# A new issue table, loads spread, minima given anew to POOL or ScalarE, and a ring of 1536 columns, in an attention and ELU kernel

## The chip, the cores and the metric

The kernel runs on one core of a Trainium2 chip. TensorE (PE; its weight loads are listed as PEld), VectorE (DVE), ScalarE (ACT), GpSimd (POOL) and SyncE (SP, which here only issues transfers) each work through a queue of their own, in its order, and wait for each other through semaphores. The metric is the device time of one execution in microseconds; for a kernel the median of its runs is given.

## The reference

Attention over a sliding window, and then two matrix products with an ELU between them. Cut to what matters:

```python
batch, n_heads, seq, head_dim = (8, 8, 576, 64)
scores = scale * np.matmul(q, k.transpose(0, 1, 3, 2))
mask = (rel >= 0) & (rel < 128)
scores = np.where(mask, scores + bias[None], -1e9)        # bias = -slope(head) * |rel|
attn = np.exp(scores - max) / (sum + 1e-09)
x = (attn @ v) as [4608, 512]                             # heads side by side
h = x @ w_in                                              # [4608, 2048]
g = np.where(h > 0.0, h, np.exp(np.minimum(h, 0.0)) - 1.0)
out = g @ w_out                                           # [4608, 512], float32
```

## The kernel before, in words

*Attention.* A batch is worked in four units (keys in blocks of 128, each with up to 256 queries). For batches 2 to 7 a unit is one run of score matmuls on four groups of 32 rows (`scores`, its matmuls recorded at L222), three exponentials on ScalarE (`expo`, L230 and L233) and two products with the table of bias and mask on VectorE (`weigh`, L238). Then come the products with v (`values`, `all_values`, L250 and L271); a column of ones beside v gives the sums. VectorE takes the reciprocal and writes a normalised block of x (`xn`). Batches 0 and 1 take a quicker way in (L136 to L213): their q and k are turned by TensorE, their bias is added by matmuls (L167, L184), and their scores use 64 rows (L177, L192).

*x turned.* The first layer needs x with its 512 features down the partitions. `xT` is a ring of columns, one column a token; a token's place is its number modulo RING, 1728 before. The first nine blocks are turned by TensorE and copied (`turn_x`); the other 31 by a transposing transfer from SyncE's queue (`turn`, L287), which also issues the stores of the output.

*First layer.* 144 hidden steps, each one PSUM bank (`hp`) of 512 values: from step 32 on, 256 tokens by two of the 16 feature groups, in eight matmuls of 256 columns (L312). A step that runs over the ring's end is cut in two pieces (`cuts` in `hidden`), and each piece has matmuls of its own. Steps share two banks in turn, so that step n+2 waits until step n's bank has been read. The ELU is max(exp(min(h, 0)) - 1, h), and exp(min(h, 0)) comes in two ways: by ScalarE alone (relu of -h, L319, then exp of its negative, L321), or by ScalarE's exp (L323) and then the minimum with 1 on POOL (L325). The set SOFT says which step goes which way. VectorE finishes (`elu`, L333), reading `e` and the bank, and frees the bank.

*Second layer.* For every 256 tokens seven products of half matrices instead of eight (Strassen's way): `product` (L403), eight matmuls for one product; the sums of g that they need on VectorE (`sums`, L364: S1 to S4), their results kept by ScalarE (`keep`, L410) and put together by VectorE (`combine`, `lower`, L364).

*Loads.* POOL issues them all: per batch eight pieces of q and k into a staging tile (`load_qk`, L108) and five of v (`load_v`, L114). POOL's minima stand in the same queue.

*The order* is written out. Each kind of work has a queue of jobs; SCRIPT is a text whose letters are taken one by one, and each letter issues the next job of its kind. What each engine does, and in which order, follows from it alone. The letters: f and fA/fD turn q and k of the first batches and copy them; b, i, j are their bias, scores and exponentials; k scores; x, y, z exponentials; w, W products with the table; v, r, n values, reciprocal, block of x; t, tA/tD and T turn x; h, p, q, e are a hidden step's matmuls, its first pass, its second pass and its end; s1 to s4 sums; o one matmul of a product, u its keeping; c and m put together and store; l the next load; C four copies of table parts.

Of the kernel before, what the change touches and what calls it, by code (L numbers as in the profile page):

```python
# [18 lines left out]
def kernel(  # L19
# [15 lines left out]
    RING = 3 * S  # L35
# [114 lines left out]
    with tc.manual_schedule():  # L150
# [369 lines left out]
        for b in range(2, B):  # L520
# [16 lines left out]
        SOFT = {15 + 8 * n + d for n in range(2, 2 * NTB) for d in (0, 1, 2, 3, 4, 7)} | set(range(11, 19)) | {20, 22, 23} | set(range(16 * NTB - 10, 16 * NTB + 8))  # L537

        SCRIPT = """
            f fD f fD b f fA f fD C C C C b i j i j j b i j j v r n v r n b t tD v r n v r n  # L540
            h p q t tD f fA
            e h p q i j f fD f fA f fD b b i j i l
            h p q e j j l
            h p q e b i l
            h p q j v r n v r n e l
            h p q t tD b i j e l
            h p q e
            h p q e
# [12 lines left out]
            s2 W l l o1 u o6 v r n i j i j j
            l l o2 c1 o5 v r n
            W W d l o3 u o4 t tA i j v r n
            W l s4 o4 u o3 v r n
            h p q v r n i j d l
            h p q e W t tA d l o5 u o2
            h p q e v r n i j l
            h p q e W t tA l o7 c2
            h p q e v r n i j d l
            h p q e W l o7 u  # L570
            h p q e v r n v r n l c3 m s1
            o1 h o2 p o1 k l q o1 e o1 v y l t tA d o1
            h x r n e o1 T o1 p o4 s2 u
            h q w o2 e o2 z o4 d p o1
            h w q c1 o2 p v e o4 q o1 r
            h s3 u n o2 p o2 e o1 T o1 u k s4 q o1
            h x e d o2 p o3
            h w u q y l o1 z e o4 p o2 d o1
            h d q w l o1 e v p o2 c2 l o1 q o1
            h r n l o1 e o1 T p o2 l o2 s1 o1 q k l u o1 e o1 x  # L580
            h l d o2 p o1 s2 o4 u
            h w q y e o4 z o2 c3 o2 p o2 w m
            h q c1 v u e p o4 s3 o1 q o1
            h r n o2 p o1 e o1 T o1 k q s4 u
            h e x d o3 p o2 w o1
            h y q z l o1 e o1 u o3 p o1 w o2
            h q d l o1 v c2 p e o1 l o2 q o2 r o2 v l u e v o2
            h r l s1 n o2 p o2
            h r T n q n o2 p e k u d o1 q o3
            h x s2 e o2 p o3 w o3 q o1  # L590
            h c1 y e o1 z o2 s3 o2 p o3 w o1
            h u q c3 v m e T o3 u o2 r o1 p s4 o3
            h n q o1 e T o1 p k d u q
            h x l e o2 p o1 w o4 z o1 q
            h c2 y l e o2 p o2 w l o4 q
            h s1 l e o1 v l p o2 r o1 q l
            h n u d o2 p k e q o3 s2 o2 u
            h x e s3 o2 p o3
            h w q c1 y o1 e o4 z o2 c3 o2 p o1 s4
            h m T u w q o4 e v u p o2 r o3 n o1 q o1  # L600
            h T e o3 u k p c3 q
            h x l e o2 p o2 w o3 y o1 q
            h c2 z l e o2 p o2 w l o2
            h q s1 l v e p l o2 r o1 u v d q o1 m l o1
            h e o1 n o1 p o4 v r T q s2 o3
            h u e o1 s3 o1 p o2
            h r n q c1 o2 n p o3 e o1 T o2 q k d u
            h x e s4 o2 p o1
            h w z d q o5 u o2 e o1 p o4 y o2 q o1
            h u w o1 e o1 p o3 v c3  # L610
            h q r n l o2 e p o1 T o2 l o2 s3 q k l u c2
            h x e m l o3 p
            h w l q s1 l o2 z o2 e o3 y o5 p o1 w
            h q s2 v u e p o4 c1 o1 q
            h r n o2 e p o1 T o4 u s4 k q
            h x e d o2 p o3
            h w u q o1 y o1 e o4 p o2 d o1
            h z q u w l o2 p o3 e o2 v q
            h l r e o1 l n o1 p o5 s3 l T q k c2 u l e
            h x l o2 p o1 w o1  # L620
            h l q s1 o1 z o1 e o4 y o2 c3 o2 p
            h w m q s2 o1 v u p o1 v r o1 e o2 q o1 v c1 o3 e o1
            h u n o2 r p o1 T o1 n
            h r q n o2 T p e o3 k u s4 q
            h x e o2 d o1 p o4
            h z w q y e o2 u o2 p o2 w o4 q
            h c2 l e o2 p v l o2 r o2 s1 q o1
            h l u n o1 l o1 e p o1 T o2 k d l q o1
            h x e o2 p o1 w
            h u s2 q o3 z o1 e o4 y o2 c3 o1  # L630
            h p w m q c1 o1 v e o4 u o2 r o1 p
            h n q s3 T k p e o2 q o1 d o3
            h x e o1 s4 u o3 p
            h w z q o3 l u o1 e o2 p o4 y o1 c2 o1 q o1
            h w l v e p l o2 r o2 c3 o1 l o1 u
            h n q l s1 T m o2 p k e l q s3 o1
            h l x e l o1 s2 o1 p o5 d u o2 q o1
            h z e o1 y o2 w o2 p o2
            h w q c1 o2 e p v v q r o2 s4 o1
            h u e o2 n p v o3 r o1 q T o1 n o3 r o1 u o1 n o1  # L640
            h u e T d o1 k p o1 q x
            h e o2 p o1 w o4 y
            h q c2 z l e o2 p o3 w l o3 q
            h s1 l e o2 p v l o2 r o1 u
            h s2 q l n o2 p o2 c3 o3 u e o1 m T q k d
            h x e o2 p o1 w o1
            h q c1 o1 z o1 e o4 y o2 s3 o2 p
            h w q o2 v u e p o3 s4 o1 u o2
            h q r n o2 p o1 e o1 T o1 k q d
            h x e o2 u o1 w o1 p o5 y o1 q o3 z  # L650
            h e c3 o2 p
            h c2 w q o3 p v e u o2 r o1 q o1 m o1 n
            h s1 T o1 k p e u d q o3
            h x s2 e o2 p o4 c1 o1 z o2 s3 o1
            h q y e o3 p o2 w o2 u o2
            h q w e o2 p v s4 o1 u o1 v q r o2 r v
# [191 lines left out]
```

## Time and profile before

| what | value |
|---|---|
| median of three runs | 305.14 us (304.5 to 305.21) |
| span of the profiled execution, first to last instruction | 303.2 us; the page gives no other time for it, and the runs' median lies 1.9 us above |
| granted TensorE clock | 1.000 |
| busy: PE, DVE, ACT, POOL | 296.2, 256.2, 238.2, 109.1 us |
| POOL's minima (L325) | 44, 28.9 us |
| ScalarE's second passes (L321) | 100, 63.6 us |

The page's span is the time on the core; what lies between it and a run's time is start and end around the program. A row of a group gives line, engine, operation, what it writes and reads, shape and count, then busy time and the mean of one in ns, then the idle time of that engine before it and who ended it. A row of the timeline starts with its start and its length in us.

### The profile page before, as it was taken

The numbers are of one execution on the slowest core, as the hardware profiler recorded it, in microseconds if no ns is written. First come the engines' busy times: TensorE is split into PE (matmuls) and PEld (weight loads), VectorE is DVE, ScalarE is ACT, GpSimd is POOL, SyncE is SP. The second block draws the span as 40 slices with busy tenths as digits, with TensorE's granted clock in tenths as the row PEclk, the third lists the DMA queues.
The fourth block names the chain that finished last, engine by engine and source line by source line (L and its number), as shares of the span: only waits on it lengthen the run. The fifth ranks groups of instructions, "written<-read, shape, count | busy, mean of one in ns | idle before, by whom it ended". The sixth has DMA issues, their size and how long they took to land.

```text
span 303.2 us, 9837 instructions
## 1 busy us (share of the span) xinstructions
PE 296.2 (98%) x4074; PEld 255.6 (84%) x4074; DVE 256.2 (85%) x499; ACT 238.2 (79%) x445; POOL 109.1 (36%) x163
## 2 busy tenths in 40 slices
PE   7899999999999999999999999999999999999996
PEld 5688876989888889988888888887899888898885
DVE  5747879989999999799989898989989887885873
ACT  5577688869797888877979888888887888868881
POOL 8947958671534243332534162606000100010000
PEclk9999999999999999999999999999999999999999
DMA  8999999999394949491969695999220301111013
GB/s 99 193 198 201 201 178 192 125 128 101 36 160 72 131 78 119 83 184 21 161 60 130 107 118 66 130 144 125 61 89 2 97 17 54 54 56 43 37 57 118
DMA packets 96941, 32.04 MB, mean 106 GB/s; under 512 B 83968, under 2 KB 92800, under 8 KB 96896
## 3 DMA queue, kind: packets, MB, share of 16 engines
q0 software_dynamic: 75920, 18.36, 66.6%
q1 hardware_dynamic: 20832, 12.98, 18.0%
q8 instruction: 32, 0.52, 0.7%
q14 instruction: 13, 0.11, 0.1%
q10 hardware_dynamic: 144, 0.07, 0.1%
HBM read 36.70 MB, written 9.44 MB: 152 GB/s over the span
## 4 chain that ended last, share of the span: by engine, by line
PE 86%; DVE 4%; DMA 4%; ACT 2%; POOL 2%; issue 1%; POOLq 0%; DVEq 0%; ACTq 0%
PE hp L312 38%; PE op L403 15%; PE av L403 14%; PE spa L222 4%; PE spa L271 3%; DMA VP<-in_v_dram 2%; PE sp L403 2%; PE sp L312 2%; DMA xT<-xn 2%; PE sp L250 1%; DVE g L333 1%; PE op L339 1%; PE spa L339 1%; ACT e L323 1%; DVE xn L259 1%
## 5 line engine op out<-in xcount | busy, mean ns | idle before, releaser
L312 PE MATMUL hp<-xT,wi 128*128 128x256 f16 (+3 forms) x1488 | 144.1, 245 | 0.9 <-DMA xT<-xn 0.4
L312 PEld LDWEIGHTS <-wi 128*128 128x128 f16 x1600 | 120.6, 98 | 15.1 <-issue 3.9
L333 DVE SCALAR_TENSOR_TENSOR g<-e,hp 128x512 f16<-128x512 f32 x138 | 93.9, 681 | 23.4 <-ACT e L321 12.0
L325 POOL TENSOR_SCALAR e<-e 128x512 f32<-128x512 f32 x44 | 28.9, 657 | 151.4 <-ACT e L323 148.6
L319 ACT ACTIVATE e<-hp 128x512 f32<-128x512 f32 x98 | 58.7, 599 | 28.2 <-PE hp L312 22.9
L321 ACT ACTIVATE e<-e 128x512 f32<-128x512 f32 x100 | 63.6, 636 | 2.2
L403 PEld LDWEIGHTS <-S 128*128 128x128 f16 x544 | 51.0, 98 | 6.6 <-issue 1.1
L403 PEld LDWEIGHTS <-g 128*128 128x128 f16 x400 | 37.1, 98 | 5.4 <-issue 1.5
L238 DVE TENSOR_TENSOR EX<-EX,TAB 128x1024 f16<-128x1024 f16 x48 | 33.0, 694 | 2.8 <-ACT EX L233 1.3
L114 POOL DMA_DIRECT2D VP<-in_v_dram x40 | 34.4, 874 | 1.7 <-DMA s<-in_k_dram 1.3
L323 ACT ACTIVATE e<-hp 128x512 f32<-128x512 f32 x40 | 24.2, 605 | 12.1 <-PE hp L312 12.0
L403 PE MATMUL op<-T,S 128*128 128x256 f16 x192 | 29.5, 273 | 0.0
L403 PE MATMUL av<-T,S 128*128 128x256 f16 x176 | 27.0, 273 | 0.0
L233 ACT ACTIVATE EX<-sp 128x512 f16<-128x512 f32 x48 | 27.0, 602 | 0.0
L230 ACT ACTIVATE EX<-spa 128x1024 f16<-128x1024 f32 x24 | 24.5, 1022 | 1.0 <-PE spa L222 0.5
L364 DVE TENSOR_TENSOR S<-g 128x1024 f16<-128x1024 f16 (+2 forms) x35 | 23.1, 666 | 0.3 <-PE op L403 0.2
L403 PE MATMUL op<-wo,g 128*128 128x256 f16 x128 | 20.4, 273 | 0.0
L403 PE MATMUL av<-wo,g 128*128 128x256 f16 x120 | 19.7, 273 | 0.0
L108 POOL DMA_DIRECT2D st<-in_k_dram x24 | 16.3, 687 | 2.9 <-DMA s<-in_q_dram 2.0
L279 DVE TENSOR_TENSOR xn<-spa,rden 128x512 f16<-128x512 f32 x24 | 16.5, 687 | 0.4
L108 POOL DMA_DIRECT2D st<-in_q_dram x24 | 15.9, 666 | 1.3 <-DMA VP<-in_v_dram 1.3
L222 PE MATMUL spa<-QT,KT 32*128 32x256 f16 (+2 forms) x240 | 15.1, 250 | 0.0
(137 smaller groups left out, 381.5 us busy)
## 6 DMA issues: line engine op xcount, KB each, us to landing
out_dram<-ob SPq DMA_DIRECT2D x32, 256.0 KB, 3.2
VP<-in_v_dram POOLq DMA_DIRECT2D x32, 128.0 KB, 6.1
st<-in_k_dram POOLq DMA_DIRECT2D x24, 144.0 KB, 5.3
st<-in_q_dram POOLq DMA_DIRECT2D x24, 144.0 KB, 5.9
wi<-in_moe_w_in_dram POOLq DMA_DIRECT2D x4, 512.0 KB, 11.2
wo<-in_moe_w_out_dram POOLq DMA_DIRECT2D x4, 512.0 KB, 10.8
out_dram<-ob SPq DMA_DIRECT2D x7, 128.0 KB, 1.7
VP<-in_v_dram POOLq DMA_DIRECT2D x8, 64.0 KB, 6.1
```

What stands on the lines that cost most here:

```text
L108: nc.gpsimd.dma_start(st[b][32 * g:32 * g + 32, w, :, :, :, :].rearrange("p h n j d -> p (h n) (j d)"), (q, k)[w][b, 2 * g:2 * g + 2, :, : ...
L114: nc.gpsimd.dma_start(VP[b % 2][0:p, n, :, 0:D], v[b, :, 128 * n:128 * n + p, :].rearrange("h p d -> p h d"))
L222: nc.tensor.matmul(sp[g][:, 256 * h2 + o:256 * h2 + o + n], kt_[b % 2][r, k0:k0 + 255:2], qt_[b % 2][r, c0:c0 + 2 * n - 1:2], start=dh == ...
L233: nc.scalar.activation(unit(b, u)[:, g, :, :], sp[g].rearrange("p (h c) -> p h c", h=2), AF.Exp, scale=0.125)
L238: V.tensor_tensor(out=e, in0=e, in1=TAB[:, int(u == 3), 2 * gp:2 * gp + 2, :, :], op=ALU.mult)
L312: nc.tensor.matmul(p[:, l * w + u0:l * w + u1], w_in_sb[:, c, fc * 128:(fc + 1) * 128], xT[:, c, x0:x0 + u1 - u0], start=(c == 0), stop=(c ...
L319: nc.scalar.activation(e[:, 0:n], p[:, 0:n], AF.Relu, scale=-1.0)
L321: nc.scalar.activation(e[:, 0:n], e[:, 0:n], AF.Exp, scale=-1.0)
L323: nc.scalar.activation(e[:, 0:n], p[:, 0:n], AF.Exp)
L325: nc.gpsimd.tensor_scalar(out=e[:, 0:n], in0=e[:, 0:n], scalar1=1.0, scalar2=0.0, op0=ALU.min, op1=ALU.max)
L333: V.scalar_tensor_tensor(out=gs[t][:, f0:f0 + nf, c0:c0 + w], in0=sh(es.pop((t, c0, f0))), scalar=1.0, in1=sh(hps.pop((t, c0, f0))), op0=A ...
L403: nc.tensor.matmul(o, a[:, j, :], b[:, j, :], start=j == 0 and i in (1, 2, 5), stop=j == 7, skip_group_check=True)
```

## The change

The whole of SCRIPT is written anew, RING becomes 1536, a turned block that runs over the ring's end is split into two transfers, and SOFT becomes a text with a letter for each of the 144 steps in their order: "a" for ScalarE alone, "g" for POOL. "a" stands 44 times, "g" 100 times; before it was 100 and 44. The jobs themselves and their queues stay as they were. A letter that stands for a load is now more often alone between other letters from batch 4 on. The four table copies C stand later.

```diff
-    RING = 3 * S
+    RING = 1536
...
-            nc.sync.dma_start_transpose(out=xT[:, :, o:o + n], in_=x[0:n, :])
+            for r0, r1 in [(0, n)] if o + n <= RING else [(0, RING - o), (RING - o, n)]:
+                c = (o + r0) % RING
+                nc.sync.dma_start_transpose(out=xT[:, :, c:c + r1 - r0], in_=x[r0:r1, :])
...
-        SOFT = {15 + 8 * n + d for n in range(2, 2 * NTB) for d in (0, 1, 2, 3, 4, 7)} | set(range(11, 19)) | {20, 22, 23} | set(range(16 * NTB - 10, 16 * NTB + 8))
+        SOFT = "aggagaaggggaggaaagaagagaggagggggagggggggaggggggagaggggagagggagaggggggggggggggggagggaaggggggaaggggggaagggggggaagagaaggggggggagggggagaggaaaagaagaa"
...
-            h x e o2 p o1 w o4 z o1 q
-            h c2 y l e o2 p o2 w l o4 q
...
+            h p r n k e o2 u u
+            h z l l o6 s1 s2 q e o2
...
-        for s in sorted(HID):
-            parts(hidden(*HID[s], s in SOFT), "h", "p", "q")
+        for n, s in enumerate(sorted(HID)):
+            parts(hidden(*HID[s], SOFT[n] == "a"), "h", "p", "q")
```

Three places of the order, before and then now. The lines of the changed kernel are 2 higher from `turn` on: L335 is `elu`, L327 the minimum, L299 the copy of a turned block.

ScalarE at the start, from the exponentials of the first two score banks on (EX_92 is the second unit, hp_101 and hp_102 the two banks of the first hidden steps, sp_100 and sp_99 two score banks):

```order
L200 ACTIVATE EX_92<-av 128x4x128
L323 ACTIVATE e<-hp_101 128x512
L141 COPY QT_85<-sp_100 128x4x128
L323 ACTIVATE e<-hp_102 128x512
L198 ACTIVATE EX_92<-spa 128x8x128
L141 COPY KT_87<-sp_99 128x2x320
L205 ACTIVATE EX_93<-spa 128x2x512
L323 ACTIVATE e<-av 128x512
```

```order
L200 ACTIVATE EX_92<-av 128x4x128
L141 COPY QT_85<-sp_100 128x4x128
L321 ACTIVATE e<-hp_101 128x512
L323 ACTIVATE e<-e 128x512
L198 ACTIVATE EX_92<-spa 128x8x128
L325 ACTIVATE e<-hp_102 128x512
L141 COPY KT_87<-sp_99 128x2x320
L205 ACTIVATE EX_93<-spa 128x2x512
L325 ACTIVATE e<-av 128x512
```

The copy of q went ahead of hidden step 0, the exponential of block 1 ahead of step 1, and step 0 has both its passes on ScalarE.

TensorE at hidden step 48, the first that ran over the ring's end (a weight load and a matmul each time):

```order
L312 LDWEIGHTS wi
L312 MATMUL hp_102<-xT,wi 128x192
L312 LDWEIGHTS wi
L312 MATMUL hp_102<-xT,wi 128x192
L312 LDWEIGHTS wi
L312 MATMUL hp_102<-xT,wi 128x192
L312 LDWEIGHTS wi
L312 MATMUL hp_102<-xT,wi 128x192
L312 LDWEIGHTS wi
L312 MATMUL hp_102<-xT,wi 128x64
```

The changed kernel has no piece of 192 columns at all, and 896 matmuls of 128x256 into the hidden banks instead of 768; TensorE issues 3946 matmuls instead of 4074.

POOL, from the loads of batch 6 (`load_qk`, then `load_v` into VP_89) on:

```order
L108 DMA st<-in_k_dram 32x18x128 x2
L108 DMA st<-in_q_dram 32x18x128 x4
L325 TENSOR_SCALAR e<-e 128x512 x2
L114 DMA VP_89<-in_v_dram 128x8x64 x4
L114 DMA VP_89<-in_v_dram 64x8x64
```

```order
L108 DMA st<-in_k_dram 32x18x128
L327 TENSOR_SCALAR e<-e 128x512
L108 DMA st<-in_q_dram 32x18x128
L327 TENSOR_SCALAR e<-e 128x512 x3
L108 DMA st<-in_q_dram 32x18x128
L327 TENSOR_SCALAR e<-e 128x512
L108 DMA st<-in_q_dram 32x18x128
L327 TENSOR_SCALAR e<-e 128x512
L108 DMA st<-in_q_dram 32x18x128
L327 TENSOR_SCALAR e<-e 128x512 x2
L114 DMA VP_89<-in_v_dram 128x8x64
```

Minima stand between the loads now, one to three at a time.

More of the change, by code (lines that the diff above doesn't have):

```diff
@@ new lines @@
+            f f fD fD b b f f fA fD i j b i v r v n r i n j j j b l l t tD j v v r n f
+            fA
+            h p r n q t tD i j f
+            h p q f fA e f b b fD fD e i i
+            h j C p C b j j i j C
+            h
+            h q e v r v
+            h b p p q p n r n t q q e i j l tD
+            h p q e e v r n l l l
+            h v v e
+            h
+            h p p r n t O p tA r n v q q e e q
+            h p
+            h p e
+            h p O q e
+            h O q e
@@ new lines @@
+            h d tA r n v v q e r p q o3 c3 r
+            h n u n k e
+            h p q s1 x v c2 o2 e p r n o4 w t q e
+            h o1 s2 l y o3 z w p o1 q e u
+            h l p q tA o10 v o3 u
+            h d d p q e
+            h p q r n k x z y O2 c1 l o7 d e o1 e
+            h l p s3 u
+            h o2 s4 o4 q p o6 q o4 T T u d d e
+            h s3 o1 p o4 e w w
+            h v m o3 c2 l q e p o2
+            h p q r n k T l u o1 l e s1 s2 s4 q e l l y
+            h o1 x w o8 u o4 c3 o2 c1 z w o4 p q e
@@ new lines @@
+            h p o2 u o1 v r n o1 l T o2
+            h p k y q q e z d l
+            h p q l o2 l d d e o6 u o8 s3 u o1
+            h o5 e o2 x
+            h c3 w w p p q c2 o1 e v q o5 v v r u n s1
+            h o1 p e o2 r n o3 m o4 u r n s2
+            h p k q e o4 c1
+            h o3 l l q o4 x l z w y p q o1 u o8 u l T o4 w v e
+            h e r p q n
+            h p k s4 x e q o3 m o1 e T T o6
+            h l o2 d u o1
+            h z o7 c2 p q y l l p q o4 d u o1 e
+            h p q o5 w w v o2 u e
@@ new lines @@
+            h p q s1 r o4 e
+            h p n k y x s2 o1 z o5 e l c1 s3 o3 l q e
+            h p
+            h l q c3 o7 T u o7 u w w v e
+            h p p o1 u s4 o2 r n k y x l l q q e e s3 o3 d o1
+            h p T l q o1
+            h o5 p o4 c2 o5 u e z d q e s1 o3 u o2 l l
+            h
+            h c3 o2 p s2 m q e w p q o4 l c1 e o5 w s4 o3
+            h p o4 q e u o2
+            h v v v r n r T o4 p
+            h o4 u p q e q l
+            h p o2 n r n k d e o3
+            h s3 o5 d T q u o5 e
@@ new lines @@
+            h p q
+            h e p k x o6 q e c1 o2 w
+            h
+            h y z w p o6 d o1 p q q e v v o1 r n r o3 e o2 u
+            h s4 v u p q o8 u r
+            h n n p q o3 T o2 e
+            h p q d d o2 k x s3 o1 y o1 z e e o5 l
+            h p q T
+            h p q l c3 o2 c2 o8 w w v u u e o4
+            h p r e
+            h n k T o1 m s1 o1 s2 q p q e o2 c1 e o2 x w o3
+            h y z o1 p q o7
+            h w u p o2 s4 o4 e
+            h q m e p q v T r n o3 u e
@@ new lines @@
+            h k o2 s3 T
+            h o5 p q e x o2 u c3 o3 p
+            h z o4 y o1 l c2 q p e
+            h p q q w o2 w v o4 e
+            h s1 l l o1 r u o5 u e
+            h p p o1 n k y z x T o3 s2 o5 s4 q e q e
+            h o2 p c1 w w q e o3
+            h p l q u o7 d e v v r r v r
+            h o1 n n u n
+            h p p o3 d o2 q q o2 u k y e e s1 o2 x m w
+            h p z l o3
+            h o1 q o3 c2 p o3 l o9 e
+            h q w v u e
+            h p o1 q o4 p T r n o3 k u o3 q s2 e e
@@ new lines @@
+            h
+            h y z s3 o5 l o2 c3 m p o1 c1 o1 T q o2 e o3 p o1 q x o1
+            h p e
+            h w w s4 v r n u o8 u o3 p k o1 T o4 z q q e e
+            h
+            h x s1 u o4 y o4 c2 w p w o3 s2 q p o2 q e e v r u o3 u o1 c3 m T
+            h p
+            h p n q s4 q k y z e o8 e
+            h
+            h c1 o3 s3 p o6 p o6 u q q e e x o1 w w
+            h
+            h o1 p q o3 e u T v v p q r e o1 s1 o3 u n v
+            h p
+            h o15 q e p
+            h q r e s2 c2
@@ new lines @@
+            h u o1 p q p o1 s3 q o9 e u o1 c3 m o1 r o1 T o2 e
+            h o1 p q n n
+            h c1 p q e e o12 u o3 u T
+            h o2 s4 p q o1
+            h p q e e o8 u o3
+            h o3 p o1
+            h s1 c2 o11 q p q s2 c3 e e o3 u u
+            h
+            h p q p q e e o5 s4 o8 m o1 c1 o1
+            h p q s3 o1
+            h o3 u p q e o11
+            h u o6 e
+            h s3 o3 u o2 p q o1 e o1 s1 P o2 p q e o1 s2 o2 s1 s2 U c2 u c4 s4 P P P U U c1 P P c2
+            U c4 Z
```

186 lines of the change are left out of this document (33 added, 153 removed).

## The prediction

> **What bounds the kernel now.** I read the page's head and its chain of waits first, then the busy time in stretches of 20 us, then who waited for whom.
>
> ```profile
> span 303.2 us, 9837 instructions
> PE 296.2 (98%) x4074; PEld 255.6 (84%) x4074; DVE 256.2 (85%) x499; ACT 238.2 (79%) x445; POOL 109.1 (36%) x163
> ...
> PE 86%; DVE 4%; DMA 4%; ACT 2%; POOL 2%; issue 1%; POOLq 0%; DVEq 0%; ACTq 0%
> ```
>
> TensorE is busy for 98% of the span and holds 86% of the chain. The next engine, VectorE, has 15% to spare. So a new order can win only what TensorE waits, and what its stream is shortened by. The stretches (length, then busy time of PE, PEld, DVE, ACT, POOL) say where it waits:
>
> ```profile
> 0.00:20.00 20.00, 16.84 (x325) 13.27 (x326) 12.56 (x35) 11.64 (x21) 15.35 (x31) 1.00 1.24 159
> ...
> 40.00:60.00 20.00, 19.70 (x337) 15.52 (x336) 18.41 (x37) 16.45 (x29) 13.57 (x19) 1.00 1.94 165
> ...
> 80.00:100.00 20.00, 19.94 (x262) 17.11 (x260) 18.89 (x37) 15.18 (x29) 10.06 (x15) 1.00 0.98 100
> 100.00:120.00 20.00, 20.00 (x268) 17.35 (x267) 18.94 (x36) 17.69 (x33) 5.96 (x9) 1.00 1.03 119
> ...
> sum 300.00, PE 295.82 PEld 255.43 DVE 255.69 ACT 238.22 POOL 109.09; mean PE 19.72 PEld 17.03 DVE 17.05 ACT 15.88 POOL 7.27
> ```
>
> Of 300 us TensorE is seen idle for 4.2: 3.2 in the first 20 us, 1.0 after that. Short waits hide, since a matmul's modelled span runs past the next one's start; the weight loads show some of them (us in total, times, longest):
>
> ```profile
> PEld L222 <- issue: 4.8, 23, 0.2
> PEld L312 <- issue: 3.9, 16, 0.6
> PEld L403 <- issue: 2.6, 12, 0.2
> ...
> PE hp L312 <- DMA xT<-xn: 0.4, 1, 0.4
> ```
>
> 4.8 over 23 is 0.21 us at each entry into the score matmuls of four row groups (L222, 24 units). 28 waits at L312 and L403 follow; if 24 of them are the way back at the same 0.2, 4.8 of their 6.5 us belong to that switch too, which the change keeps. What is left, 1.7 us, and the 1.0 of visible idle overlap in part: **an order can win 1.0 to 2.7 us after the start**, not more.
>
> **The change, part by part.**
>
> *Ring of 1536.* A hidden step whose 256 columns cross the ring's end runs 16 matmuls instead of 8. 1728 is crossed by steps 48 to 55 (192+64), 3456 by steps 104 to 111 (128+128): 16 steps, 128 matmuls. 1536 is six times 256, so none is cut. Three pieces of the chain (start, length) and a transfer:
>
> ```profile
> 108.64 0.87 PE hp L312 x8
> ...
> 112.16 0.89 PE hp L312 x16
> ...
> 127.66 0.89 POOL e L325
> ...
> 200.42 4.68 DMA xT<-xn
> ```
>
> A whole step takes 0.87, a cut one 0.89: 16 x 0.02 = **-0.3 us**. The other bound would be the 128 weight loads themselves, if they weren't hidden, but 0.89 for sixteen shows that they are; nothing from there. One transpose, that of batch 5, block 1, becomes two; its second half lands one issue later. The order leaves 5.9 us of matmuls between its input and step 88, the landing on the chain took 4.7, and there is 1.2 for the issue: just enough, so nothing; late, it costs that issue at most.
>
> *The start.* The row that matters is the wait for the copies of the third part of q and k:
>
> ```profile
> 14.41 0.44 PE L136 MATMUL sp<-ident,s 64*64 64x64 f16 x16
> 16.58 1.02 ACT L198 ACTIVATE EX<-spa 128x1024 f16<-128x1024 f32 x1
> 16.85 0.82 DVE L141 COPY KT<-av 128x640 f16<-128x640 f16 x1 [0.81 <-PE av L136]
> 17.59 0.95 DVE L141 COPY QT<-hp 128x768 f16<-128x768 f16 x1
> 18.61 0.33 PEld L177 LDWEIGHTS <-KT 64*128 64x128 f16 x8 [0.21 <-DVE QT L141]
> ...
> 21.82 1.07 PE L312 MATMUL sp<-xT,wi 128*128 128x128 f16 x16
> ```
>
> Now the 16 transposes of 14.41 stand ahead of step 0, ScalarE copies q before it touches step 0, and the scores of block 1 and the transposes into av stand ahead of step 1. Step 0 ends 0.28 later (14.2 with its tail); its two ScalarE passes (0.60 and 0.64) and its 0.69 on VectorE end near 16.2. VectorE then copies k (0.82, to 17.0) and q (0.95, to 17.97), and L177 starts at 18.05 instead of 18.61. The exponential behind it starts 0.55 earlier, but step 3 now comes after the next scores, so by step 4 (21.82) **-0.4** is left. Bounds: -1.0, if step 3 fits in the shadow of that exponential, and +0.5, if VectorE takes the copies later than I walked it. The four table copies that leave the idle 8.5 to 10.3 us cost VectorE 1.9 us later on, spread over 18 to 50 us; 40 to 60 us, its fullest part, has 1.6 of 20 to spare: nothing, as long as it has.
>
> *The order after the start.* The one long wait for the transpose (0.4, with 4.68 of DMA on the chain at 200.42) should go: from the last attention matmul of that block to step 96 there are 7.5 us of matmuls before and 8.7 in the change, and the smallest such distance of all blocks rises from 5.1 to 7.1. Of 1.0 to 2.7 I take **-1.5**. One more switch into and out of the 64-row scores stands in the order (18 pairs, not 17): **+0.2**.
>
> *The minima.* Shape, count, busy time, mean in ns, idle before and its cause; the last row has the least, the middle and the longest duration:
>
> ```profile
> L333 DVE SCALAR_TENSOR_TENSOR g<-e,hp 128x512 f16<-128x512 f32 x138 | 93.9, 681 | 23.4 <-ACT e L321 12.0 <-POOL e L325 8.4 <-PE hp L312 1.1
> L321 ACT ACTIVATE e<-e 128x512 f32<-128x512 f32 x100 | 63.6, 636 | 2.2
> L238 DVE TENSOR_TENSOR EX<-EX,TAB 128x1024 f16<-128x1024 f16 x48 | 33.0, 694 | 2.8 <-ACT EX L233 1.3 <-ACT EX L230 1.2
> L325 POOL TENSOR_SCALAR e<-e 128x512 f32<-128x512 f32 x44 | 28.9, 657 | 151.4 <-ACT e L323 148.6 <-issue 2.4
> L364 DVE TENSOR_TENSOR S<-g 128x1024 f16<-128x1024 f16 x33 | 22.3, 681 | 0.3 <-PE op L403 0.2
> ...
> L325 POOL TENSOR_SCALAR e<-e x44: 602/612/1107, 14.7 to 267.1; 128x512 f32<-128x512 f32 x44
> ```
>
> 56 steps go from ScalarE to POOL: ScalarE 238.2 - 56 x 0.636 = 202.6 us, POOL 109.1 + 56 x 0.657 = 145.9. ScalarE isn't the bound, so its 35.6 us are worth only the waits counted above. The way of one step gets longer. A POOL step, then a ScalarE step:
>
> ```profile
> 203.04 1.04 PE L312 MATMUL hp<-xT,wi 128*128 128x256 f16 x8
> 204.12 0.60 ACT L323 ACTIVATE e<-hp 128x512 f32<-128x512 f32 x1
> 204.87 0.65 POOL L325 TENSOR_SCALAR e<-e 128x512 f32<-128x512 f32 x1 [1.15 <-ACT e L323]
> 205.55 0.69 DVE L333 SCALAR_TENSOR_TENSOR g<-e,hp 128x512 f16<-128x512 f32 x1 [0.17 <-POOL e L325]
> ...
> 290.01 1.04 PE L312 MATMUL hp<-xT,wi 128*128 128x256 f16 x8
> 291.08 0.60 ACT L319 ACTIVATE e<-hp 128x512 f32<-128x512 f32 x1
> 291.71 0.63 ACT L321 ACTIVATE e<-e 128x512 f32<-128x512 f32 x1
> 292.38 0.69 DVE L333 SCALAR_TENSOR_TENSOR g<-e,hp 128x512 f16<-128x512 f32 x1
> ```
>
> From the matmuls' end to the bank's release: 206.24 - 204.08 = 2.16 us by POOL, 293.07 - 291.05 = 2.02 by ScalarE. The matmuls that the change puts between two steps on one bank last 2.34 us at the least behind a POOL step (2.51 at 0.109 each, less the 0.17 by which a step's end trails), 2.18 behind a ScalarE step. So a minimum that runs on time costs nothing, and one that is over 0.2 late can stop TensorE. What makes one late is VectorE:
>
> ```profile
> 57.62 0.67 DVE L213 TENSOR_TENSOR EX<-EX,TAB 128x1024 f16<-128x1024 f16 x1
> 57.67 1.11 POOL L325 TENSOR_SCALAR e<-e 128x512 f32<-128x512 f32 x1 [0.25 <-ACT e L323]
> ...
> 80.61 0.60 POOL L325 TENSOR_SCALAR e<-e 128x512 f32<-128x512 f32 x1
> 80.81 0.95 DVE L238 TENSOR_TENSOR EX<-EX,TAB 128x1024 f16<-128x1024 f16 x1
> ```
>
> Whichever begins second stands until the other is done: the minimum of 57.67 takes 1.11 instead of 0.61, the product of 80.81 takes 0.95 instead of 0.68. The mean of 657 against the middle one's 612 makes 44 x 0.045 = 2 us of lateness now; 100 minima make 4.5. Two of 44 stood on the chain (127.66 is one, late by 0.27): 4 or 5 of 100, at 0.1 to 0.27 each, half of it in slack: **+0.5**. Bounds: nothing, and the rival below.
>
> The Trainium skill (SBUF — State Buffer, section Who interferes with whom) says that a DVE instruction with two SBUF inputs contends with a GpSimd instruction that reads SBUF, and that whoever issues first has the shared ports for the whole instruction. The four rows above agree. It speaks against more minima on POOL, and applied to a table that takes no care of it, it gives the slower rival's time.
>
> *Loads spread* between minima: a minimum waits at most for an issue of 0.7 to 0.9 us; by the order these sit where the next step on the bank is 4 us away. Nothing.
>
> **Sum:** -0.3 - 0.4 - 1.5 + 0.2 + 0.5 = -1.5: a span of 301.7. The runs' median, 305.14, is 1.9 above the profiled span; carried over, **303.6 us**.
>
> **Rivals.** *All the room is taken:* 2.7 after the start, 1.0 in it, no loss to POOL: 305.14 - 0.3 - 1.0 - 2.7 + 0.2 = 301.3. For it: every tight distance of the old order that I counted got longer. Against: the shared ports, which no order sees. *Late minima eat the gain:* ring and start hold, the order's 1.5 is returned by minima: 304.6 to 305, no change. *VectorE becomes the bound through the ports (the slower side):* some 150 of its instructions read twice from SBUF (48 products of L238, 33 sums of L364 and 33 of its like, the rest smaller). POOL would hold a minimum for 100 x 0.61 = 61 of 303 us, a fifth; 150 x 0.2 x half of 0.61 = 9 us more on VectorE, 0.75 in each of 12 stretches. 80 to 120 us has 1.1 to spare in 20, which delays of that size use up; if half of the 9 stops TensorE and the order gains nothing, 305.14 - 0.7 + 4.5 = 309. It decides from 19.5 us of VectorE in 20. Against: the 48 products' mean is 694 now, so that all of them together lost 1 us at most against the 0.67 of an undisturbed one. *The ring does nothing*, because a cut step costs 0.02: that is in the sum already.
>
> **Chances.** Forecast (302.3 to 304.6) 0.44, all room 0.18, no change 0.2, slower 0.18. A measurement of this kernel can tell about 0.3% (0.9 us) from no change, so faster means under 304.2: 0.39 of the forecast and the 0.18, with 0.02 of the third, 0.59; slower means over 306.1: 0.18 and 0.02 of the third, 0.20; the same 0.21. The range leaves out half of the slower case and a little of the best: 300.4 to 307.4.
>
> **What would show it.** Right: no 192-wide piece under hp<-xT; L177's first row near 18.05; no wait of hp for xT; ACT near 203, POOL near 146 or a little more, its minimum's mean near 660 to 700; L238's mean up by some 10 ns. Wrong: VectorE over 19.5 in a stretch, PE waiting for g (L335) many times, a minimum's mean over 750, or a PE idle in the first 20 us above 3.2.

## The result, and the profile after

The change made the kernel slower: 308.31 us (308.16 to 308.51, four runs) against 304.82 us before (304.43 to 305.21), a ratio of 1.0116, interval 1.0101 to 1.013. A second comparison (the twelfth experiment) gave 1.0115, 1.0096 to 1.0134. The forecast was 303.6 us with a range up to 307.4. Times are medians of all runs of a kernel, while ratios and intervals leave out the few runs that fell into a slower state (one of e4, one of e6, two of e17 and one of the kernel before).

The head of the page and the chain of waits of the changed kernel:

```profile
span 306.4 us, 9546 instructions
PE 298.6 (97%) x3946; PEld 254.5 (83%) x3946; DVE 261.7 (85%) x499; ACT 210.0 (69%) x389; POOL 147.5 (48%) x219
...
PE 75%; DVE 11%; DMA 5%; issue 4%; POOL 2%; ACT 2%; DVEq 0%; POOLq 0%; ACTq 0%
```

POOL gained 38 us, about as worked out (36.8). ScalarE lost 28.2 and not 35.6: the durations of its instructions, added up, did fall by 35.6 us (265.4 to 229.9), but neighbours overlap in the record (290.07 + 0.63 ends behind 290.61 in the trace of before), and busy time counts an overlap once. VectorE, whose list of instructions is the same 499 as before, is busy 5.5 us longer (256.2 before), and its share of the chain went from 4% to 11% while TensorE's fell from 86% to 75%. Which instructions grew is seen in the groups by shape (count, busy us, mean ns). Three groups of before that are not shown above, then those of the changed kernel:

```profile
L364 DVE TENSOR_TENSOR S<-g,S 128x1024 f16<-128x1024 f16 x17 | 11.5, 677 | 0.0
L364 DVE TENSOR_TENSOR S<-S,g 128x1024 f16<-128x1024 f16 x16 | 10.7, 671 | 0.0
...
L364 DVE TENSOR_TENSOR ob<-U,U 128x256 f32<-128x256 f32 x17 | 7.0, 413 | 2.3 <-ACT U L410 2.3
```

```profile
L335 DVE SCALAR_TENSOR_TENSOR g<-e,hp 128x512 f16<-128x512 f32 x138 | 92.8, 678 | 21.7 <-POOL e L327 14.3 <-ACT e L323 6.4
L238 DVE TENSOR_TENSOR EX<-EX,TAB 128x1024 f16<-128x1024 f16 x48 | 34.7, 748 | 1.1 <-ACT EX L230 0.5 <-ACT EX L233 0.3
L366 DVE TENSOR_TENSOR S<-g 128x1024 f16<-128x1024 f16 x33 | 24.3, 735 | 1.0 <-PE av L405 0.5
...
L366 DVE TENSOR_TENSOR S<-S,g 128x1024 f16<-128x1024 f16 x16 | 12.9, 803 | 0.2
L366 DVE TENSOR_TENSOR S<-g,S 128x1024 f16<-128x1024 f16 x17 | 12.6, 743 | 0.1
L366 DVE TENSOR_TENSOR ob<-U,U 128x256 f32<-128x256 f32 x17 | 7.8, 460 | 0.1
...
L327 POOL TENSOR_SCALAR e<-e 128x512 f32<-128x512 f32 x100 | 67.9, 680 | 138.3 <-ACT e L325 137.8
```

The groups that read twice from SBUF while minima run grew (L238 was at 694; a sum at some 680, a combine of two U at 413), and the mean of no other group rose by more than 10 ns: the activation of L335, which reads one operand from PSUM, stands at 678 against 681. The minimum's mean rose only from 657 to 680. One place, 132 us in, in order of time, the three engines one after another (start, length):

```profile
132.20 0.69 DVE L335 SCALAR_TENSOR_TENSOR g<-e,hp 128x512 f16<-128x512 f32 x1 [0.23 <-ACT e L323]
132.81 1.09 DVE L238 TENSOR_TENSOR EX<-EX,TAB 128x1024 f16<-128x1024 f16 x1
133.83 0.41 DVE L366 TENSOR_TENSOR ob<-U,av 128x256 f32<-128x256 f32 x1
134.16 0.68 DVE L335 SCALAR_TENSOR_TENSOR g<-e,hp 128x512 f16<-128x512 f32 x1
134.75 0.68 DVE L238 TENSOR_TENSOR EX<-EX,TAB 128x1024 f16<-128x1024 f16 x1
135.36 1.09 DVE L366 TENSOR_TENSOR S<-g,S 128x1024 f16<-128x1024 f16 x1
136.37 0.68 DVE L335 SCALAR_TENSOR_TENSOR g<-e,hp 128x512 f16<-128x512 f32 x1
...
132.75 0.60 POOL L327 TENSOR_SCALAR e<-e 128x512 f32<-128x512 f32 x1 [1.85 <-ACT e L325]
...
134.83 1.07 POOL L327 TENSOR_SCALAR e<-e 128x512 f32<-128x512 f32 x1 [0.60 <-ACT e L325]
...
133.06 1.04 PE L314 MATMUL hp<-xT,wi 128*128 128x256 f16 x8
134.94 1.04 PE L314 MATMUL hp<-xT,wi 128*128 128x256 f16 x8
...
137.21 1.04 PE L314 MATMUL hp<-xT,wi 128*128 128x256 f16 x8
```

The minimum of 132.75 runs on time (0.60), and the product that starts 0.06 behind it takes 1.09 instead of 0.68. The next minimum starts behind a product, is late (1.07), and in turn stretches the sum of 135.36. The activation of 136.37, for which TensorE's next step on that bank waits, comes two stretches late. A meeting is an overlap in time of a minimum and such an instruction in which one of the two lasts over 60 ns longer than its like. Counted over the whole trace, 28 of the 100 minima stand in a meeting that stretched VectorE (24 of its instructions, 16 of them sums or combines), and 13 more were late themselves; before, the 44 minima stretched four instructions, and never a sum.

TensorE's own rows hardly show the loss. None of its waits of 0.2 us or more is for g, and from 20 to 290 us it is seen idle for 1.3 us, against 1.0 before. Its busy time rose instead, to 298.6 us, though it has 128 matmuls fewer: the recorded end of a matmul is modelled, and short waits between matmuls are covered by it.

### The profile page after: what moved, and what is told of

The parts are those of the page before. It is cut to its first block, busy times and chain, and to the rows that moved or that the text cites. A ratio compares the mean times of both kernels' runs of the same rounds, so it can differ in the third digit from the quotient of the medians.

```text
span 306.4 us, 9546 instructions
## 1 busy us (share of the span) xinstructions
PE 298.6 (97%) x3946; PEld 254.5 (83%) x3946; DVE 261.7 (85%) x499; ACT 210.0 (69%) x389; POOL 147.5 (48%) x219
## 4 chain that ended last, share of the span: by engine, by line
PE 75%; DVE 11%; DMA 5%; issue 4%; POOL 2%; ACT 2%; DVEq 0%; POOLq 0%; ACTq 0%
PE hp L314 33%; PE op L405 14%; PE av L405 13%; DMA VP<-in_v_dram 5%; PE spa L222 4%; PE spa L271 3%; DVE g L335 3%; DVE EX L238 2%; PE sp L405 2%; DVE S L366 2%; DVE ob L366 1%; PE sp L250 1%; POOL e L327 1%; PE sp L314 1%; PE av L250 1%
## 5 line engine op out<-in xcount | busy, mean ns | idle before, releaser
L314 PE MATMUL hp<-xT,wi 128*128 128x256 f16 (+2 forms) x1360 | 139.7, 252 | 0.3
L327 POOL TENSOR_SCALAR e<-e 128x512 f32<-128x512 f32 x100 | 67.9, 680 | 138.3 <-ACT e L325 137.8
L314 PEld LDWEIGHTS <-wi 128*128 128x128 f16 x1472 | 117.0, 98 | 14.1 <-issue 2.3
L335 DVE SCALAR_TENSOR_TENSOR g<-e,hp 128x512 f16<-128x512 f32 x138 | 92.8, 678 | 21.7 <-POOL e L327 14.3
L238 DVE TENSOR_TENSOR EX<-EX,TAB 128x1024 f16<-128x1024 f16 x48 | 34.7, 748 | 1.1 <-ACT EX L230 0.5
L323 ACT ACTIVATE e<-e 128x512 f32<-128x512 f32 x44 | 27.7, 631 | 1.3
L366 DVE TENSOR_TENSOR S<-g 128x1024 f16<-128x1024 f16 (+2 forms) x35 | 25.1, 717 | 1.0 <-PE av L405 0.5
L405 PE MATMUL av<-T,S 128*128 128x256 f16 x176 | 25.0, 273 | 0.3 <-DVE ob L366 0.2
L405 PE MATMUL op<-wo,g 128*128 128x256 f16 x128 | 18.6, 273 | 0.0
L405 PE MATMUL av<-wo,g 128*128 128x256 f16 x120 | 18.1, 273 | 0.0
L412 ACT COPY U<-op 128x256 f32<-128x256 f32 x32 | 11.9, 373 | 8.2 <-PE op L405 7.7
```

Source lines behind the costliest of these rows:

```text
L238: V.tensor_tensor(out=e, in0=e, in1=TAB[:, int(u == 3), 2 * gp:2 * gp + 2, :, :], op=ALU.mult)
L314: nc.tensor.matmul(p[:, l * w + u0:l * w + u1], w_in_sb[:, c, fc * 128:(fc + 1) * 128], xT[:, c, x0:x0 + u1 - u0], start=(c == 0), stop=(c ...
L323: nc.scalar.activation(e[:, 0:n], e[:, 0:n], AF.Exp, scale=-1.0)
L327: nc.gpsimd.tensor_scalar(out=e[:, 0:n], in0=e[:, 0:n], scalar1=1.0, scalar2=0.0, op0=ALU.min, op1=ALU.max)
L335: V.scalar_tensor_tensor(out=gs[t][:, f0:f0 + nf, c0:c0 + w], in0=sh(es.pop((t, c0, f0))), scalar=1.0, in1=sh(hps.pop((t, c0, f0))), op0=A ...
L366: V.tensor_tensor(out=o, in0=a, in1=b, op=op)
```

## The experiments

Theory A: the time goes where POOL's minima and VectorE's instructions with two SBUF inputs meet. Theory B: the new order is worse by itself, wherever the minima stand. Smaller suspects were the tail, the start and the ring. Each ratio is to the kernel before, timed beside it on the same chip.

**Is it the reading? A POOL instruction that only writes (e4, e5).**

```diff
-                nc.gpsimd.tensor_scalar(out=e[:, 0:n], in0=e[:, 0:n], scalar1=1.0, scalar2=0.0,
-                                        op0=ALU.min, op1=ALU.max)
+                nc.gpsimd.memset(e[:, 0:n], 1.0)          # e4; e5: e[:, 0:n + 96] of a 608-wide tile
```

> The changed kernel with POOL's minimum replaced by a write of ones into the same tile: the minimum with 1 is left out (so the steps given to POOL compute max(h, 0) only), the wait for ScalarE before it and VectorE's wait after it stay, and POOL reads nothing from SBUF. Theory A, the ports are taken by a POOL instruction that reads SBUF: no VectorE instruction with two SBUF inputs is stretched, VectorE falls to 252 to 255 us, the time to 305 to 306.2. If the longer way through a third engine is what costs: VectorE falls the same, the time stays at 307.5 or more. If POOL's writes take the ports as well: VectorE stays near 260 and the time near 308.

> As the run with the memset (the minimum with 1 is left out, POOL writes ones and reads nothing), but the write covers 608 columns instead of 512, so that it lasts about as long as a minimum on time (612 ns) instead of 525. Theory A, the ports: what was won came from the meetings, not from the shorter instruction; no VectorE instruction is stretched, VectorE stays at 254 to 256 us, the span is 301 to 302.5. If the 87 ns that the memset is shorter by made the gain (100 x 0.087 = 8.7 us of POOL): the span goes back to 304.5 or above though nothing is stretched.

Both kernels leave out the minimum with 1, so that they compute something else than the reference; waits, order and places stay. e4: 304.67 us, ratio 0.999 (0.9956 to 1.0024). e5: 303.95 us, 0.9971 (0.9949 to 0.9993). Of e5:

```profile
span 303.0 us, 9542 instructions
PE 295.0 (97%) x3946; PEld 254.3 (84%) x3946; DVE 255.1 (84%) x499; ACT 209.5 (69%) x389; POOL 138.2 (46%) x219
...
L327 POOL MEMSET e<- 128x608 f32 x100 | 60.5, 606 | 144.1 <-ACT e L325 142.3 <-issue 1.4
L238 DVE TENSOR_TENSOR EX<-EX,TAB 128x1024 f16<-128x1024 f16 x48 | 31.6, 684 | 1.6 <-ACT EX L230 0.7 <-ACT EX L233 0.6
```

At the length of a minimum on time (606 ns), in the same places, behind the same waits, it stretches nothing: 56 times such a write overlaps a VectorE instruction with two SBUF inputs, and none of these is stretched; L238 is back at 684, VectorE at 255.1. From 1.0115 to 0.9971 is 1.4%, **4.4 us**; that e4's write is shorter has no part in it that these runs can tell.

**Which meetings? (e13 to e16).** The same write of 608 columns, now only at some of the 100 steps:

```diff
+                if soft == "m":
+                    nc.gpsimd.memset(e[:, 0:n + 96], 1.0)
+                else:
                     nc.gpsimd.tensor_scalar(out=e[:, 0:n], in0=e[:, 0:n], scalar1=1.0, scalar2=0.0,
```

> The changed kernel in which only the 41 minima that met a VectorE instruction with two SBUF inputs in its trace (either of the two over 60 ns late) are replaced by the write of ones of 608 columns (their minimum with 1 is left out); the other 59 are the minima as they were. Theory A, the price is the meetings: as the fifth experiment, 303.5 to 304.8, VectorE 254.5 to 257. If something else of a POOL that reads SBUF costs the time (a slower ScalarE write, a slower DMA), its 59 minima bring most of it back: 306 to 307.

> The complement: the 59 minima that met nothing are replaced by the write of ones of 608 columns, the 41 that met stay. Theory A: 308.0 to 308.6, VectorE 261 to 262, as the changed kernel. If the replacement itself wins time wherever it stands: 305.5 to 306.5.

> Only the 28 minima in whose meeting VectorE was stretched are replaced by the write of ones of 608 columns. If VectorE's 8.6 us are the price (the prediction's rival): 304.3 to 305.5. If the late minima are (the prediction's own term, put at 0.5 us): 307 or more.

> Only the 13 minima that were late themselves, with nothing of VectorE stretched behind them, are replaced by the write of ones of 608 columns. If VectorE's stretch is the price: 307.3 to 308.3, VectorE at 261 to 262. If the late minima are: 305.5 or less.

| steps with the write | time | ratio | VectorE busy |
|---|---|---|---|
| the 41 that met (e13) | 304.02 | 0.9969 (0.9949 to 0.999) | 255.3 |
| the 59 that met nothing (e14) | 307.78 | 1.0103 (1.0069 to 1.0137) | 261.4 |
| the 28 with VectorE stretched (e15) | 303.77 | 0.9971 (0.9946 to 0.9997) | 254.8 |
| the 13 with the minimum alone late (e16) | 307.72 | 1.0093 (1.0067 to 1.0119) | 261.6 |

With the 28 alone replaced, the time is that of all 100 replaced (e5): as far as these runs can tell, the 28 are the whole price. e15's groups hold 72 real minima, and their mean is still 659, but VectorE's rows are those of an undisturbed engine:

```profile
L330 POOL TENSOR_SCALAR e<-e 128x512 f32<-128x512 f32 x72 | 47.4, 659 | 113.7 <-ACT e L325 113.4
...
L238 DVE TENSOR_TENSOR EX<-EX,TAB 128x1024 f16<-128x1024 f16 x48 | 31.6, 684 | 1.6 <-ACT EX L230 0.7 <-ACT EX L233 0.6
L369 DVE TENSOR_TENSOR S<-g 128x1024 f16<-128x1024 f16 x33 | 22.8, 691 | 1.0 <-PE av L408 0.5
...
L369 DVE TENSOR_TENSOR S<-g,S 128x1024 f16<-128x1024 f16 x17 | 11.6, 680 | 0.1
L369 DVE TENSOR_TENSOR S<-S,g 128x1024 f16<-128x1024 f16 x16 | 11.0, 685 | 0.2
```

Late minima cost little or nothing: e16 lies 0.7 us under the unaltered change, but their intervals overlap, and two of the 24 stretches of VectorE are gone in its trace too. The traces of the change and of e15 have the same 144 activations in the same order, so they can be laid side by side. How much later each ends in the changed kernel (worked out from the rows of L335 and L338), at some steps; a star marks one of the 28:

```
step       33    35*   39*   42    57*   58*   64*   73*   82*   97*   104*  120*  143
lag, us  0.24  1.14  1.32  1.01  1.59  2.00  2.39  2.83  3.18  3.57  3.93  4.22  4.05
```

The lag grows at most of the starred steps and nearly nowhere else, by up to 0.6 each (6.2 us over all 28); 2.4 us are given back between them. The place shown above, in e15:

```profile
132.23 0.42 DVE L369 TENSOR_TENSOR ob<-U,av 128x256 f32<-128x256 f32 x1
132.56 0.68 DVE L338 SCALAR_TENSOR_TENSOR g<-e,hp 128x512 f16<-128x512 f32 x1
133.16 0.69 DVE L238 TENSOR_TENSOR EX<-EX,TAB 128x1024 f16<-128x1024 f16 x1
133.76 0.69 DVE L369 TENSOR_TENSOR S<-g,S 128x1024 f16<-128x1024 f16 x1
134.36 0.68 DVE L338 SCALAR_TENSOR_TENSOR g<-e,hp 128x512 f16<-128x512 f32 x1
...
131.88 1.04 PE L314 MATMUL hp<-xT,wi 128*128 128x256 f16 x8
...
135.69 1.04 PE L314 MATMUL hp<-xT,wi 128*128 128x256 f16 x8
```

From the first of these activations to the second 1.80 us, in the changed kernel 2.21; TensorE's step that began 1.18 later before (133.06 against 131.88) begins 1.52 later behind it (137.21 against 135.69).

**Order and minima taken apart (e1, e2, e8).** e1 and e2 exchange the lists of minima between the two orders; e8 is e1 with both ScalarE passes in one place.

```diff
-        SOFT = "aggagaaggggagg..."                          # e1: the list of before; e2: this list in the order of before
+        SOFT = "ggggggggggggaaaaa..."
...
-                yield                                        # e8: no yield between the two ScalarE passes of a step
```

> The changed kernel, its order and ring, with the minima given as before (44 on POOL, 100 on ScalarE). Theory A, the ports: the loss comes from the 100 minima on POOL that meet VectorE's instructions with two SBUF inputs; with 44 of them VectorE's busy time falls from 261.7 us to 254 to 257, PE's share of the chain comes back over 82%, and the time to 305 to 306.2 (305.1 less 0.3 for the ring, plus the 0.5 lost in the start and the 0.9 of the tail). Theory B, the order itself: the time stays at 307.5 or above, with VectorE's busy time down all the same.

> The kernel before, its order and ring, with the changed kernel's list of minima (100 on POOL, 44 on ScalarE, by the number of the step). Theory A, the ports: 25 or so of VectorE's instructions are stretched by 0.3 us each, VectorE goes from 256.2 to 260 or more, and the time to 307 to 309. Theory B, the order itself: 304.4 to 305.6, as before; VectorE may lose its 8 us without anything waiting for it.

> The changed kernel with the minima as before (44 on POOL, 100 on ScalarE), like the first experiment, but each step that goes from POOL to ScalarE runs its two ScalarE passes in one place, where the new order has the first. The first experiment's second pass stood where POOL's minimum did, behind other steps' first passes and copies, so 337.8 may say only that a ScalarE order was spoilt. If so, this one comes to 305 to 308. If ScalarE's time itself is short in the new order (its passes come in bunches of two steps), it stays over 312.

e1: 337.8 us, 1.1081 (1.1047 to 1.1115). e2: 314.57, 1.0324 (1.03 to 1.0348). e8: 318.29, 1.045 (1.0425 to 1.0475). Theory A's numbers failed on all three, by up to 32 us; so did theory B's for e2. For e8 the other branch came out (over 312), which put the loss down to ScalarE's time in the new order; but ScalarE isn't full there (15.0 to 16.7 us in 20 from 80 to 160 us), so this isn't shown. In e1 TensorE waits for the activation 21 times, up to 2.4 us, in e2 nine times:

```profile
PE hp L314 <- DVE g L335: 20.0, 21, 2.4
```

```profile
PE hp L312 <- DVE g L333: 4.3, 9, 1.2
```

The traces do settle one thing. The number of stretched instructions goes with the list and not with the order: the new list has 24 in its own order and 24 in the order of before (e2, VectorE at 261.6), the old list has 4 in its own and 6 and 5 in the new one (e1, e8). But e2 loses more than twice as much as the change. So neither list's time can be judged in the other's order: a table of this kind is one plan, in which a step's second pass has its place among the rest. What the meetings cost these runs don't tell; the replacements above do.

**Buying the meetings off (e6, e10, e11, e17).** e6 gives the 41 minima that met to ScalarE, both passes in one place; e10 leaves them on POOL and puts the activation that waits for the minimum ahead of the instruction that it would stretch, at 23 places; e11 adds the tail of before and a merged store; e17 gives seven steps alone to ScalarE, and merges the store.

> The changed kernel with the 41 minima that met an instruction of VectorE in its trace (one of the two lasted over 60 ns too long) given to ScalarE, both ScalarE passes in one place of its order; 59 minima stay on POOL. Theory A, the ports, with ScalarE in no need of its time: meetings fall to 10 or fewer, VectorE to 255 to 257 us, the time to 304 to 305.5. If the new order can't bear a second pass on ScalarE in these places (it was laid out for one), ScalarE's instructions and the copies of U behind them come late and the time is 308 or above, with PE waiting for U or for g behind ScalarE.

> The changed kernel with VectorE's order mended at 23 places: where an instruction with two SBUF inputs was stretched by a minimum, the activation step (L335) that waits for this same minimum now comes ahead of it (with its minimum and ScalarE's first pass ahead too, where the table had them behind). Nothing goes to another engine. Theory A, the ports: the instructions stretched fall from 24 to 10 or fewer, VectorE from 261.7 to 257 or less, the steps' activation comes 0.5 us earlier in these places, and the time falls by 1.5 to 3 us to 305.3 to 306.8. If VectorE, which now idles until the minimum is done instead of standing in front of the ports, is late with its other work all the same: 307.5 or more.

> The kernel of the tenth experiment with the tail of the kernel before (seventh experiment) and the merged store (ninth). If the three gains add up: 0.5 to 1.2 us under the tenth experiment, 304.3 to 306. If the tail is hidden behind the stores' landing: as the tenth, within 0.5.

> The changed kernel with seven of the 28 minima that stretch VectorE (steps 39, 57, 58, 68, 70, 82, 102) given to ScalarE, both passes in one place, and the two stores merged as in the ninth experiment. The seven are those places where the sixth experiment's trace lost less time than the changed kernel's against the fifteenth: step by step the difference is 0.4, 0.75, 0.36, 0.34 and 0.3 us, 1.8 to 2.1 in all, and 0.5 for the store. If the losses stand by themselves, place by place: 305.7 to 306.3, VectorE near 259.5. If ScalarE's longer passes shift what meets what elsewhere: 307 or more. Under 304, which would beat both kernels, neither theory puts it.

e6: 310.86, 1.0198 (1.0173 to 1.0223), though VectorE is at 256.1 and one instruction alone is stretched. e10: 317.95, 1.0443 (1.0401 to 1.0485); e11: 318.33, 1.0442 (1.042 to 1.0465). e17: 307.4, 1.007 (1.0042 to 1.0097). Of e10, groups and waits:

```profile
L335 DVE SCALAR_TENSOR_TENSOR g<-e,hp 128x512 f16<-128x512 f32 x138 | 93.6, 681 | 33.7 <-POOL e L327 25.6 <-ACT e L323 6.9 <-ACT e L325 0.3
L238 DVE TENSOR_TENSOR EX<-EX,TAB 128x1024 f16<-128x1024 f16 x48 | 33.4, 714 | 0.8 <-ACT EX L233 0.3 <-ACT EX L230 0.3
```

```profile
PE spa L271 <- DVE EX L238: 4.7, 9, 1.0
```

VectorE is busy 3.8 us less than in the change (257.9), but its activations stand idle for POOL 25.6 us instead of 14.3, and the products and sums that were put behind them come late: the values matmuls wait for a product nine times. In this order the swaps cost more than the stretches that they avoid. e6 has four waits of TensorE for a copy of U (1.4 us) that the change doesn't have, and 2.5 us of waits for VectorE's products and activations; where the rest of its loss lies isn't shown. e17, chosen place by place from the lags, won about 0.45% of the 1.15%, some 1.4 us where 2.0 to 2.6 were expected, the merged store included. Why a part of the gain is missing isn't shown. No version that computes the whole reference came out under the kernel before.

**Ring and tail (e3, e9, e7).** e3 is the kernel before with the ring of 1536 and the split transpose; e9 also merges two neighbouring stores of the last but one tile; e7 is the change with the last products and combines in the order of before.

```diff
-                if n == 2 * NTB - 2:
-                    put(n, 1, 0, 256)
-                put(n, 1, 256 if late else 0, DO)
+                put(n, 1, 256 if n == 2 * NTB - 1 else 0, DO)
```

> The kernel before with the ring of 1536 columns and the split transpose alone. By the prediction's term 305.14 - 0.3 = 304.8, a ratio of 0.999. If the reuse of the ring's columns after 3 batches less 192 columns makes a transpose wait for a reader, 305.5 or more, with a wait of PE hp for xT of over 0.4 us.

> The kernel before with the ring of 1536, as in the third experiment, and the two stores of the second half of the last but one tile's rows merged into one, so that SyncE issues one DMA fewer and the last store uses the same one of its 8 semaphores as in the kernel before. In the third experiment's trace SyncE's waits at the end stood 0.45 us longer, since the last store's semaphore was looked at second and seven others after it at 0.06 us each. If that is the ring's loss: from VectorE's last instruction to the span's end 2.5 us instead of 3.0, and the time 0.4 to 0.5 under the third experiment's 305.7, that is 305.2. If the ring's loss sits elsewhere: no change, 305.5 or more.

> The changed kernel with the last products and combines in the order of the kernel before (P U U P c1 U P c4 c2 Z instead of P U U c1 P P c2 U c4 Z): c4, which waits for no late product, comes ahead of c2 on VectorE. If the tail is worth what the two traces show (2.8 us from the last matmul's end to the span's end before, 3.7 after): the time goes down by 0.5 to 0.9 us, to 307.4 to 307.8. If the landing of the last store sets it: no change, 308.1 to 308.5.

e3: 305.72, 1.0035 (1.001 to 1.006): no gain, rather a loss of 1.1 us. e9: 304.84, 1.0011 (0.999 to 1.0031). e7: 308.32, 1.0131 (1.0096 to 1.0167), as the change itself: the tail's order is worth nothing that these runs can tell. The matmuls are gone as worked out (1360 in L314's group against 1488), but at the end of e3's trace SyncE's looks at the semaphores of its transfers stand so:

```
before  last issue 300.70 to 301.03; waits 301.08 ... 301.40, 301.66, 301.96, 302.26 (the last store's, looked at last)
e3      last issue 300.46 to 300.79; waits 300.84, 302.08 (the last store's, second), then seven more, 0.06 apart, to 302.52
```

The split block adds one transfer to SyncE's queue, the eight semaphores go round by one, and the last store is no longer looked at last: seven looks that were hidden behind its landing follow it. From VectorE's last instruction to the span's end that is 3.0 us instead of 2.5 (300.44 to 303.4; 300.67 to 303.2); with one transfer fewer, in e9, it is 2.5 again (302.49 to 305.0). The change's own trace ends as e3's does. This part is seen in the traces; that e9's time is lower is borne out only by the medians, since the two intervals overlap.

**The change once more (e12).**

> The changed kernel itself, unaltered, beside the three others on the same chip: 308.3, as timed before (308.16 to 308.51). The first 20 us tell whether its late TensorE clock (matmuls slow until 6 us, L177 at 19.1 us) belongs to the kernel or to that execution: if to the execution, L177 may be anywhere from 18.2 to 19.5.

308.34 us, 1.0115. Its first scores of L177, and those of the other executions:

```profile
L177 PEld LDWEIGHTS <-KT x64: 92/94/97, 18.9 to 59.5; 64*128 64x128 f16 x64
```

```profile
L177 PEld LDWEIGHTS <-KT x64: 92/94/96, 18.2 to 58.9; 64*128 64x128 f16 x64
```

```profile
L177 PEld LDWEIGHTS <-KT x64: 92/94/97, 18.0 to 58.5; 64*128 64x128 f16 x64
```

These are the change's first profile, e12 and e15, with the same first 20 us of order: the 18.9 belongs to that execution. In it TensorE waited 0.5 us for a load of v, in the other two for no load.

## Why the prediction was wrong

**Start and order together: near the forecast, but not located.** With the 28 meetings gone the change runs at 0.9971 of before. e3 has the ring alone at 1.0035; the difference, 0.64% or 2.0 us (about 1 us to either side), is what start and order won together if the ring costs the same in both orders, against -0.4 - 1.5 + 0.2 = -1.7 in the sum. The idle time from which the order's room was worked out doesn't bear it out: from 20 to 290 us TensorE is seen idle for 1.02 us before and for 1.07 in e15, and the weight loads' waits that it counted (L222, L312, L403) add up to 11.3 us before and 11.1 in e15. What fell is the idle time of the first 20 us, from 3.16 to 2.25, and this stretch differs between executions.

**The start: right in kind, its size not settled.** L177 was forecast at 18.05 against 18.61. In the six executions of the new order in whose first 20 us TensorE is seen to wait for no load (e6, e10, e12, e13, e15, e16) it starts at 18.0 to 18.5, in the first profile, with its wait for v, at 18.9. Every execution of the order of before waits for a load there: e3 the least, 0.3 us, at 18.4; the one above at 18.6; e2 and e9, with 1.6 and 1.0 us of it, at 19.4 and 20.5. No two are alike, a gain of 0 to 0.4 us is what they allow, and that is less than one execution differs from the next.

**Loads, the transposing transfer, the switch: nothing seen against them.** No wait of a hidden step for the transpose is left.

**The ring: wrong by some 0.8 to 1.4 us.** -0.3 was forecast, and the bound named for the split transpose was "that issue at most". Of the 1.1 us that it cost in e3 (interval 0.3 to 1.8), 0.5 sits at the program's end, in a place that the walk did not look at; the rest isn't located. That the 128 matmuls saved anything is not shown: TensorE's busy time in e3 is 296.5 us against 296.2.

**The minima: the step that failed.** The term was +0.5; it measured +4.4. The prediction counted late minima, 100 instead of 44 at the lateness of before, and priced the ones that stand on the chain. Two things in it were wrong. First, it looked at the wrong side of the meeting: e15 shows that the stretched VectorE instructions are what costs, and e16 that late minima cost nothing that stands clear of the noise. The gauges named for it followed the same error: the minimum's mean came out at 680, inside the band that was to show the step right, and TensorE's waits for g, which were to show it wrong, don't appear. Two others did speak: L238's mean rose by 54 ns, where some 10 were forecast, and VectorE passed 19.5 us in a stretch. Second, the number of meetings was taken as a rate for each minimum. It depends on which steps go to POOL: four instructions stretched by 44 minima, then 24 by 100, where the rate of before gives nine, and sums among them for the first time; by e2, e1 and e8 the list makes this number, in either order. The row set against the rival (L238 at 694, "1 us at most") described the 44 minima of before only, and places for meetings could have been sought in the new listing: a w, s or c3 between a step's q and its e. Where e10 mended 23 of those, the stretched instructions fell from 24 to 11.

**The rival on the slower side was the one to back.** It had 9 us more on VectorE (6.9 measured: 261.7 against e15's 254.8), half of it stopping TensorE (4.4 of 6.9), and 309 us (308.3), with 0.18. That the time came so near is in part luck: it had -0.7 for ring and start and nothing for the order, where the runs have +1.1 for the ring and -2.0 for start and order. And its reading as a full engine is wrong. 19.5 us in 20 was to be the point from which it decides, and there are such stretches in the change:

```profile
80.00:100.00 20.00, 19.70 (x261) 17.00 (x259) 19.82 (x35) 12.08 (x24) 10.61 (x17) 1.00 0.98 109
...
140.00:160.00 20.00, 19.84 (x232) 16.53 (x223) 19.86 (x34) 14.37 (x28) 10.78 (x16) 1.00 0.88 107
```

But e15 has one too, and TensorE loses nothing in it:

```profile
80.00:100.00 20.00, 20.00 (x268) 17.58 (x266) 19.62 (x38) 12.52 (x24) 10.29 (x16) 1.00 1.02 122
```

And in e10 VectorE is less busy and the kernel 9.6 us slower. How full the engine is doesn't decide here; by the lags above, when single activations come does.

The sum with measured terms, each over the 304.5 to 304.9 of its own comparison: ring +1.1, start and order -2.0, meetings +4.4, together +3.5. The change's measured difference is the same (308.31 - 304.82), but this is no further test: the second and the third term are differences between the ratios of these same runs.

The Trainium skill's rule (SBUF — State Buffer, section Who interferes with whom) that was cited against the change held in both halves: a GpSimd instruction that reads SBUF stretched VectorE's two-input instructions, and one that only writes SBUF, which the page excepts, stretched none of the 56 that it overlapped (e5).

## What to carry to other kernels

Before giving work to POOL, list which VectorE instructions with two SBUF inputs the order puts beside it, and price the stretch on VectorE, not the lateness on POOL; the old trace's rate does not tell how often they will meet when other steps go to POOL. To find out what a suspected cost is worth, replace the instruction in its place by one of the same length without the suspected property, at chosen places only: this settled what exchanging whole lists and orders could not. When order and list were laid out as one plan, the time of an exchange is not the price of the part exchanged: here the old list (e1) made the new order 29 us slower, while it took away 18 of the 24 stretches.

## What was unexpected of the hardware

One transfer more in SyncE's queue made the end of the program 0.5 us longer, by where the last store's semaphore stands among eight that are looked at one after another. And the time that TensorE's first matmuls take is not fixed: the same 22 warming matmuls from 1.19 us on took 4.15 us in the first profile of before and 4.87 in that of the change, whose transposes were still slow at 6.4 us (op: 192 ns at the least, 234 in the middle; before, 193 in the middle).

```profile
1.19 4.15 PE L448 MATMUL op<-T 128*128 128x256 f16 x22 [1.19 <-DVE T L454]
```

```profile
1.19 4.87 PE L450 MATMUL op<-T 128*128 128x256 f16 x22 [1.19 <-DVE T L456]
...
L136 PE MATMUL op<-ident,s x16: 192/234/238, 6.4 to 6.8; 64*64 64x64 f16 x16
```

Other executions of the changed order took 4.46 (e4) to 4.88 us (e5, e12), but e12 then had L177 at 18.2, so this alone doesn't make a start late. A load can: in e5 TensorE waited 1.4 us for one of q, and L177 came at 19.9. The first 20 us of a single profile can be off by half a microsecond and more.
